# Extra products of other widths, addresses and tile forms behind the last product

## The chip, the cores and the metric

The kernel runs on one core of one Trainium2 chip. The core has five engines with a queue each: TensorE (PE for its matmuls, PEld for its weight loads), VectorE (DVE), ScalarE (ACT), GpSimd (POOL) and SyncE (SP, which issues all DMAs here). The metric is the time of one execution on the device in microseconds; the figure for a kernel is the median of its runs.

## The reference

Decayed linear attention over blocks, and then a two-layer network with a squared ReLU on the concatenated heads:

```python
batch, n_heads, seq, head_dim = (4, 8, 768, 64)      # attention
n_tokens, d_model, d_ff = (3072, 512, 2048)          # network
for b in range(nb):
    intra = np.einsum('bhic,bhjc->bhij', qb, kb) * Dmask[None]
    intra = np.einsum('bhij,bhjd->bhid', intra, vb)
    inter = np.einsum('bhid,bhde->bhie', qb * lam_pow[None], kv_state)
    out[:, :, sl] = intra + inter
    kv_state = lam_block[None, :, None, None] * kv_state + np.einsum('bhsd,bhse->bhde', kb_dec, vb)
...
h = x @ w_in
r = np.maximum(h, 0.0)
return ((r * r) @ w_out).astype(np.float32)
```

## The kernel before

The 3072 tokens are cut into 24 chunks of 128 (index t), and these into six groups of four (index m, 512 tokens). For each chunk the attention gives 512 features by 128 tokens; `split` stores them as a rounded part `xh` and a remainder `xl` in the tiles of the group, `xs_of[m]`. The network works on a group at a time: for each of the 16 slices f of the hidden layer, `hidden` makes 12 products into one PSUM tile (`wh` with `xh`, `wl` with `xh`, `wh` with `xl`, four blocks of 128 features each), `square` and `rest` make a rounded and a remaining part of the squared ReLU, and `project` makes 12 more products into the four accumulators of the group. Weights are held in `wh` and `wl`, 32 slots of 128 x 512 each, and both they and `xh`, `xl`, `gh`, `gl` have the type float32r. The attention's operands (`kv_sb`, `qk_sb`, `kv`, `a`, `mask`) are float32.

The order on each engine is that of the program text; nothing is rescheduled. In the main loop the attention of chunk t, which belongs to the next group, is spread over four slices: `scores` (line 304: 64 rows of the array for each head, two heads in different halves of the rows and different PSUM tiles), `masked`, then `attend` with `news` (line 335), `within` (line 343) and `before` (line 350), which use all 128 rows and 64 columns, two heads in different halves of the output partitions. `project` runs one slice behind `hidden`. So the last instructions of TensorE are those of `project` for the last slice of the last group: its products go two accumulators at a time (lines 428, 429, 433), and each finished accumulator is copied out by ScalarE (line 441) or VectorE (line 439) and sent by a DMA on SP (line 443). The body ends there (line 580); behind it comes the closing of the program, which the profile puts at line 630.

Other lines that are referred to: `warm` (line 65: products on a zeroed tile at the start, their results never read), `get_near` (line 248), `get_wide` (line 262) and `get_qpow` (line 278), which build tables at the start. Line 401 is the product of `hidden`.

PSUM has three pools here: `ps_acc` (four buffers, the accumulators), `ps_h` (two, the hidden slices), `ps_a` (two, named "att": scores and attention results). The last use of `ps_a` is the attention of chunk 23, in the next to last group.

Of the kernel before, what the change touches and what calls it, by code (L numbers as in the profile page):

```python
# [7 lines left out]
F32 = mybir.dt.float32  # L8
# [7 lines left out]
P = 128  # L16
B, H, S, D = 4, 8, 768, 64
# [4 lines left out]
DM = H * D  # L22
# [5 lines left out]
NM = NT // G  # L28
# [7 lines left out]
def body(ctx: ExitStack, tc: tile.TileContext, qT, kT, kvq, lam, w, out):  # L36
    nc = tc.nc
# [6 lines left out]
    ps_a = ctx.enter_context(tc.tile_pool(name="ps_a", bufs=2, space=PSUM))  # L44
    V = nc.vector
    rows = [slice(j * D, (j + 1) * D) for j in range(2)]
# [45 lines left out]
    wh = const.tile([P, 2 * NF, DM], F32R, name="wh")  # L92
# [5 lines left out]
    def w_out(f):  # L98
        return 2 * f + 2 if f < NF - 1 else 2 * NF - 1
# [97 lines left out]
    for p in range(NPR):  # L197
# [5 lines left out]
    mask = const.tile([P, 2, NPR, C], F32, name="mask")  # L203
# [5 lines left out]
        lambda o, x, y, op=op: V.tensor_tensor(out=o, in0=x, in1=y, op=op)  # L209
# [21 lines left out]
    for k in range(NS - 1):  # L231
        n = 1 << k
        x = (tr if k else s)[:, k : k + 1]
# [63 lines left out]
    xs_of = {}  # L297

    def scores(t, pool, name):
        sc_of[t] = [pool.tile([P, DM], F32, name=name) for _ in range(2)]  # L300
        k_, q_ = feat[t][:, 0], feat[t][:, 1]
        for p in range(NPR):
            for j, r in enumerate(rows):
                nc.tensor.matmul(  # L304
                    sc_of[t][j][:, p * C : (p + 1) * C], k_[r, p], q_[r, p],
                    start=True, stop=True, skip_group_check=True,
                )
# [83 lines left out]
                )  # L391


    g_of, accs, stage = {}, {}, []

    def hidden(m, f, xh, xl):
# [22 lines left out]
    def project(m, f):  # L419
        gh, gl = g_of.pop((m, f))  # L420
        if f == 0:
            accs[m] = [ps_acc.tile([P, DM], F32, name="acc") for _ in range(G)]
        end = f == NF - 1
        j = w_out(f)

        def high(i):
            cs = slice(i * C, (i + 1) * C)
            nc.tensor.matmul(accs[m][i], gh[:, cs], wh[:, j], start=f == 0, stop=False)  # L428
            nc.tensor.matmul(accs[m][i], gh[:, cs], wl[:, j], start=False, stop=False)  # L429

        def low(i):
            cs = slice(i * C, (i + 1) * C)
            nc.tensor.matmul(accs[m][i], gl[:, cs], wh[:, j], start=False, stop=end)  # L433
            if end:
                if i == 0:
                    stage.append(wk.tile([P, G, DM], F32, name="o", tag="raw"))
                o = stage[-1][:, i]
                if i % 2:
                    V.tensor_copy(o, accs[m][i])
                else:  # L440
                    nc.scalar.copy(o, accs[m][i])
                t = m * G + i
                nc.sync.dma_start(out=out[t * C : (t + 1) * C, :], in_=o)

        n = 2 if end and m == NM - 1 else 1
        for i in range(0, G, n):
            for step in (high, low):
                for k in range(i, i + n):
                    step(k)
# [81 lines left out]
    for m in range(NM):  # L531
        if m + 1 < NM:
            new_x(m + 1)
        for f in range(NF):
# [43 lines left out]
            if step == 0:  # L578
                scores(t, ps_a, "att")
    project(*prev)  # L580


def _limit():
# [50 lines left out]
```

## Time and profile before

| | |
|---|---|
| time, median of 2 runs | 636.02 us (635.94 to 636.09) |
| span of the profiled execution | 636.4 us |
| TensorE matmuls, busy | 624.6 us, 3744 instructions |
| TensorE weight loads, busy | 508.8 us, 3744 instructions |
| VectorE, ScalarE, GpSimd, busy | 222.1, 233.9, 88.5 us |
| DMA | 48.81 MB, of it 6.29 MB written to memory |

Times are in microseconds from the first instruction unless marked ns. A row of the groups of instructions has the line, engine, operation, output <- input by the program's names, the part of the array in use (rows*columns), the shape, the count, then busy time in us and the mean of one in ns, then the idle time before them and what ended it. Rows of the timeline and of the chain begin with a start and a length; "x12" counts merged instructions. The rows of one source line have the shortest, the median and the longest duration in ns, then the first and the last start. The chain is the work that ended last, followed back from the last instruction. A matmul's recorded duration reaches from its start until its result has left the array, and the next begins before that; so the cost of one in a row of matmuls is the distance from start to start.

### The profile page before, as it was taken

The page shows a single profiled execution, that of the slowest core. Times are in us where ns is not written, and L with a number is a line of the kernel's source. Part 1 is how long each engine was busy: PE and PEld are TensorE (multiplying, and loading weights), DVE is VectorE, ACT ScalarE, POOL GpSimd, SP SyncE. Part 2 cuts the span into 40 slices and gives each one's busy share as a digit, 9 for nine tenths or more (in the row PEclk, how much of TensorE's full clock was granted, in tenths as well). Part 3 has the DMA queues.
Part 4 walks back from the last instruction along what each step waited for, and adds up shares of the span by engine and source line. Part 5 has one row for each costly group of instructions (what it writes and reads, how often), then busy time and mean ns, then how long its engine had stood idle before and what let it go on. Part 6 is the DMA issues. An engine that isn't in the chain of part 4 may idle for free.

```text
span 636.4 us, 8960 instructions
## 1 busy us (share of the span) xinstructions
PE 624.6 (98%) x3744; PEld 508.8 (80%) x3744; DVE 222.1 (35%) x341; ACT 233.9 (37%) x383; POOL 88.5 (14%) x105
## 2 busy tenths in 40 slices
PE   8889999999999999999999999999999999999997
PEld 5768888888788888888888888888888888888885
DVE  6899999922222023121221221212312212211111
ACT  3277777723232324232323232323232323322232
POOL 4631222321010100210120010101201000000000
PEclk9799999999999999999999999999999999999999
DMA  8647576232021013010211202102302000100001
GB/s 310 253 134 239 161 261 205 96 131 67 1 66 52 17 67 106 27 67 2 67 57 76 67 1 76 58 1 67 122 11 67 1 2 0 67 1 1 0 1 66
DMA packets 18488, 48.81 MB, mean 77 GB/s; under 512 B 2064, under 2 KB 2064, under 8 KB 18448
## 3 DMA queue, kind: packets, MB, share of 16 engines
q1 hardware_dynamic: 18448, 48.24, 22.3%
q8 instruction: 29, 0.48, 0.3%
q14 instruction: 11, 0.09, 0.0%
HBM read 41.94 MB, written 6.29 MB: 76 GB/s over the span
## 4 chain that ended last, share of the span: by engine, by line
PE 95%; DVE 2%; DMA 1%; POOL 0%; issue 0%; ACT 0%; SPq 0%; DVEq 0%; POOLq 0%
PE h L401 40%; PE acc L428 14%; PE acc L429 14%; PE acc L433 14%; PE att L304 3%; PE att L343 3%; PE att L350 2%; PE att L335 2%; PE att L65 1%; DMA raw<-in_w 1%; DVE mask L288 1%; PE acc L304 0%; DVE A L152 0%; PE h L304 0%; PE h L248 0%
## 5 line engine op out<-in xcount | busy, mean ns | idle before, releaser
L416 DVE TENSOR_TENSOR gl<-h,gh 128x512 fp32r<-128x512 f32 x96 | 66.3, 691 | 395.8 <-ACT h L411 395.8
L408 ACT ACTIVATE h<-h 128x512 f32<-128x512 f32 x96 | 55.9, 582 | 346.8 <-PE h L401 346.7
L428 PE MATMUL acc<-wh,gh 128*128 128x512 f32 x384 | 151.7, 395 | 0.0
L429 PE MATMUL acc<-wl,gh 128*128 128x512 f32 x384 | 149.6, 390 | 0.0
L433 PE MATMUL acc<-wh,gl 128*128 128x512 f32 x384 | 149.0, 389 | 0.0
L401 PE MATMUL h<-xh,wh 128*128 128x512 f32 x384 | 105.3, 396 | 0.7 <-ACT xh L370 0.7
L401 PE MATMUL h<-xh,wl 128*128 128x512 f32 x384 | 103.0, 390 | 2.0 <-DVE wl L161 2.0
L401 PE MATMUL h<-xl,wh 128*128 128x512 f32 x384 | 102.6, 389 | 0.0
L428 PEld LDWEIGHTS acc<-wh,gh 128*128 128x128 f32 x384 | 72.1, 188 | 17.9 <-issue 2.1
L401 PEld LDWEIGHTS h<-xh,wl 128*128 128x128 f32 x384 | 72.0, 188 | 17.7 <-DVE wl L161 2.4
L433 PEld LDWEIGHTS acc<-wh,gl 128*128 128x128 f32 x384 | 72.1, 188 | 15.2
L401 PEld LDWEIGHTS h<-xl,wh 128*128 128x128 f32 x384 | 72.1, 188 | 15.0
L401 PEld LDWEIGHTS h<-xh,wh 128*128 128x128 f32 x384 | 70.5, 188 | 16.9 <-ACT xh L370 0.9
L429 PEld LDWEIGHTS acc<-wl,gh 128*128 128x128 f32 x384 | 72.1, 188 | 14.2
L410 ACT ACTIVATE gh<-h 128x512 fp32r<-128x512 f32 x96 | 57.6, 600 | 3.0
L411 ACT ACTIVATE h<-h 128x512 f32<-128x512 f32 x96 | 57.0, 594 | 0.0
L311 POOL TENSOR_TENSOR qk_sb<-qk_sb,qpow 128x512 f32<-128x512 f32 x18 | 23.3, 1295 | 200.9 <-PE att L304 200.9
L388 POOL TENSOR_TENSOR kvd<-kv,qpow 64x256 f32<-64x256 f32 x32 | 21.4, 668 | 155.9 <-DVE kv L360 86.6
L343 PE MATMUL att<-a,kv_sb 128*64 128x128 f32 x336 | 23.6, 282 | 2.5 <-DVE a L323 2.5
L323 DVE TENSOR_TENSOR a<-att,mask 128x512 f32<-128x512 f32 x40 | 25.6, 681 | 0.0
L122 ACT ACTIVATE A<-raw 128x1024 f32<-128x1024 f32 (+1 forms) x17 | 18.6, 1095 | 18.8 <-DMA raw<-in_w 15.5
L304 PEld LDWEIGHTS att<-qk_sb 64*128 64x128 f32 x320 | 19.4, 187 | 6.8 <-issue 6.7
(91 smaller groups left out, 385.3 us busy)
## 6 DMA issues: line engine op xcount, KB each, us to landing
raw<-in_w SPq DMA_DIRECT2D x32, 512.0 KB, 4.6
kv_sb<-in_kvq SPq DMA_DIRECT2D x22, 512.0 KB, 4.7
out_x<-o SPq DMA_DIRECT2D x24, 256.0 KB, 2.2
qk_sb<-in_kT SPq DMA_DIRECT2D x22, 256.0 KB, 2.6
qk_sb<-in_qT SPq DMA_DIRECT2D x22, 256.0 KB, 3.0
lent<-in_kvq SPq DMA_DIRECT2D x2, 512.0 KB, 7.6
lent<-in_kT SPq DMA_DIRECT2D x2, 256.0 KB, 7.9
lent<-in_qT SPq DMA_DIRECT2D x2, 256.0 KB, 7.3
```

Of the source, the lines that this page charges most:

```text
L304: nc.tensor.matmul(sc_of[t][j][:, p * C : (p + 1) * C], k_[r, p], q_[r, p], start=True, stop=True, skip_group_check=True,)
L311: nc.gpsimd.tensor_tensor(out=feat[t][:, 1], in0=feat[t][:, 1], in1=qpow, op=ALU.mult)
L323: V.tensor_tensor(out=a, in0=sc_of[t][j].rearrange("p (a b) -> p a b", a=NPR), in1=mask[:, j], op=ALU.mult,)
L343: nc.tensor.matmul(o[r, p * C : (p + 1) * C], tok[t][1][:, 2 * p + j, :], a[j][:, p, :], start=first and p == 0, stop=last, skip_group_che ...
L401: nc.tensor.matmul(h, wt[:, w_in(f), kt * P : (kt + 1) * P], x[:, kt], start=k == 0, stop=k == 11)
L408: nc.scalar.activation(h, h, AF.Relu)
L410: nc.scalar.activation(gh, h, AF.Square)
L411: nc.scalar.activation(h, h, AF.Square)
L416: V.tensor_tensor(out=gl, in0=r, in1=gh.bitcast(F32), op=ALU.subtract)
L428: nc.tensor.matmul(accs[m][i], gh[:, cs], wh[:, j], start=f == 0, stop=False)
L429: nc.tensor.matmul(accs[m][i], gh[:, cs], wl[:, j], start=False, stop=False)
L433: nc.tensor.matmul(accs[m][i], gl[:, cs], wh[:, j], start=False, stop=end)
```

## The change

A function `probes` is added and called once, behind the last `project`. It issues products on operands that lie in SBUF anyway: weights from `wh` (slot j, columns c to c + 127) with `xf[0]`, the `xh` of the last group seen as 128 x 2048; and, in the last loop, 64x64 blocks of `mask` with rows of `mask`. They write new "att" tiles, and nothing reads them. Every product starts its own result (start and stop both set).

```diff
+    def probes():
+        xf = [x.rearrange("p a b -> p (a b)") for x in xs_of[NM - 1]]
+        def lot(n, width, stationary, offset=0, rows_=slice(0, P), banks=1):
+            ts = [ps_a.tile([P, DM], F32, name="att") for _ in range(banks)]
+            for i in range(n):
+                j, c = stationary(i)
+                r = rows_[i % len(rows_)] if isinstance(rows_, list) else rows_
+                a = (i % 2) * DM + offset
+                nc.tensor.matmul(
+                    ts[i % banks][:, 0:width], wh[r, j, c : c + P], xf[0][r, a : a + width],
+                    start=True, stop=True, skip_group_check=True,
+                )
+        other = lambda i: (i % 32, i % 4 * P)
+        same = lambda i: (3, P)
+        lot(12, 512, other)
+        lot(12, 512, same)
+        lot(16, 256, other)
+        lot(12, 384, other)
+        lot(16, 128, other)
+        lot(12, 512, other, offset=256)
+        lot(12, 512, other, offset=32)
+        lot(16, 512, other, rows_=rows, banks=2)
+        lot(16, 256, other, rows_=rows, banks=2)
+        for width in (128, 256):
+            ts = [ps_a.tile([P, DM], F32, name="att") for _ in range(2)]
+            for i in range(32):
+                r, c = rows[i % 2], rows[i // 2 % 2]
+                nc.tensor.matmul(
+                    ts[i % 2][c, 0:width], mask[r, 0, i % 4, 0:D],
+                    mask[r, 0].rearrange("k p i -> k (p i)")[:, 0:width],
+                    start=True, stop=True, skip_group_check=True,
+                )
...
     project(*prev)
+    probes()
```

The nine calls of `lot` issue 124 products and the last loop 64, together 188. With `rows_=rows` a product uses 64 rows of the array, the lower and the upper half in turn, and writes two PSUM tiles in turn. In the last loop the row half changes with every product and the column half with every second, so that four products in a row use the four quarters of the array.

## The prediction

> **What bounds the kernel now.** The page comes first: span, busy shares, clock, and the shares of the chain that ended last.
>
> ```profile
> span 636.4 us, 8960 instructions
> PE 624.6 (98%) x3744; PEld 508.8 (80%) x3744; DVE 222.1 (35%) x341; ACT 233.9 (37%) x383; POOL 88.5 (14%) x105
> ...
> PEclk9799999999999999999999999999999999999999
> ...
> PE 95%; DVE 2%; DMA 1%; POOL 0%; issue 0%; ACT 0%; SPq 0%; DVEq 0%; POOLq 0%
> ...
> L428 PE MATMUL acc<-wh,gh 128*128 128x512 f32 x384 | 151.7, 395 | 0.0
> ```
>
> TensorE is busy for 98% of the span and makes up 95% of the chain. After the first slices its clock is granted in full. So one more matmul costs its place in the row of matmuls, unless it lies beside the tail of the program. The 395 ns of the L428 row is not that place: matmuls overlap. The chain in order of time gives the distance from one matmul to the next.
>
> ```profile
> 618.13 2.72 PE h L401 x12
> ...
> 623.57 2.72 PE h L401 x12
> ...
> 631.28 0.47 PE acc L433 x2
> ...
> 631.77 0.69 DVE o L439
> ```
>
> Twelve products of 512 columns take 2.72 us, which is 0.2267 us each. The timeline of the tail and the instructions of L630 (the end of the program) show what stands behind the last product.
>
> ```profile
> 630.79 2.43 SPq L443 DMA_DIRECT2D out_x<-o  x4
> ...
> 631.12 0.61 PE L433 MATMUL acc<-wh,gl 128*128 128x512 f32 x2
> 631.54 0.58 ACT L441 COPY o<-acc 128x512 f32<-128x512 f32 x1 [0.77 <-PE acc L433]
> 631.77 0.69 DVE L439 COPY o<-acc 128x512 f32<-128x512 f32 x1 [0.67 <-PE acc L433]
> ```
>
> ```profile
> L630 SPq EVENT_SEMAPHORE  x7: 17/28/2037, 633.3 to 636.3; - x7
> ...
> L630 SPq DRAIN  x3: 7/7/7, 635.6 to 635.9; - x3
> L630 PEldq DRAIN  x2: 13/1482/2952, 628.8 to 636.0; - x2
> ...
> L630 PEldq EVENT_SEMAPHORE  x2: 51/51/51, 635.8 to 636.3; - x2
> ```
>
> The last two products start at 631.12 and 631.35, so TensorE's next slot is 631.12 + 2 x 0.2267 = 631.57. After it come two copies, the output DMAs, and a 2037 ns wait of SP for their landing, with TensorE idle. SP's drain at 635.6 opens the closing handshake of all engines, which ends with the span at 636.4: 0.8 us. TensorE therefore has 635.6 - 631.57 = 4.0 us of free cover at the end.
>
> **The change part by part.** Nothing is removed or moved. No DMA, no VectorE, ScalarE or GpSimd instruction is added; nothing of SP's queue is passed. Behind project(*prev) stand 188 products in eleven lots, and on TensorE nothing is queued behind them but its closing drain. The operands (wh, the last xh, mask) were written long before, so no wait for another engine is expected.
>
> First, how many matmul instructions a product makes, and the price of those that are not 128x128 with 512 columns. The groups of instructions, the timeline of the start, one line's instructions and the granted clock:
>
> ```profile
> L343 PE MATMUL att<-a,kv_sb 128*64 128x128 f32 x336 | 23.6, 282 | 2.5 <-DVE a L323 2.5
> L304 PE MATMUL att<-qk_sb 64*128 64x128 f32 x320 | 23.2, 285 | 0.0
> ...
> L65 PE MATMUL att<-kv 128*128 128x512 f32 x8 | 6.6, 977 | 1.3 <-POOL kv L59 1.3
> ```
>
> ```profile
> 9.21 1.95 PE L248 MATMUL h<-pz 8*128 8x8 f32 x16
> 11.55 0.85 PE L262 MATMUL h<-near,move 128*128 128x64 f32 x6 [0.39 <-ACT near L252]
> 12.34 1.12 PE L278 MATMUL att<-blk,pz 8*128 8x512 f32 x2
> ```
>
> ```profile
> L262 PE MATMUL h<-near,move x6: 275/275/294, 11.6 to 12.1; 128*128 128x64 f32 x6
> ```
>
> ```profile
> L278 PE MATMUL att<-blk,pz x2: 587/640/692, 12.3 to 12.9; 8*128 8x512 f32 x2
> ```
>
> ```profile
> core 0: us, PE busy (x) PEld busy (x) DVE busy (x) ACT busy (x) POOL busy (x), PEclk, DMA share, GB/s
> ...
> 9.20:11.20 2.00, 1.96 (x17) 1.86 (x16) 1.81 (x3) 0.03 (x2) 0.00 (x0) 1.00 1.06 420
> 11.20:13.00 1.80, 1.45 (x8) 1.04 (x8) 0.68 (x4) 1.24 (x2) 0.00 (x0) 1.00 1.00 407
> 505.90:508.30 2.40, 2.40 (x49) 2.19 (x48) 0.51 (x1) 1.67 (x3) 0.00 (x0) 1.00 0.03 7
> ```
>
> L248 issues 8 float32 products and has 16 instructions, L278 one and has two: a float32 product is two passes. L428 has 384 for 384 float32r products: one pass. The lots on wh and xh are float32r (124 passes); the two on mask are float32 (64 products, 128 passes).
>
> Loads: at full clock (column PEclk, 1.00) the six passes of L262 with 128-column weights and 64 moving columns follow each other every (0.85 - 0.275)/5 = 0.115 us. So little streams there that the weight load sets the distance.
>
> Tiles: the L278 passes, alone in the array, start (1.12 - 0.587) = 0.53 us apart for 512 columns. With one load of 0.115 inside it that leaves 0.42, or 0.105 to 0.13 us per 128 columns. The chain shows the passes of half-width tiles:
>
> ```profile
> 506.02 0.62 PE att L335 x16
> 506.64 0.88 PE att L343 x16
> 507.51 0.87 PE att L350 x16
> ...
> 522.21 1.09 PE att L304 x16
> 523.30 2.95 PE h L401 x12
> ```
>
> L343 and L350 (128*64 tiles, 128 columns) take 0.0545 us per pass, half of a lone pass: two tiles run at once. L304 (64*128 tiles) takes 1.09 with a change of tile form at its head; without 0.22 for that it is again 0.0545. The change back shows as 2.95 against 2.72: 0.23. L335, 64 columns, gets down to 0.62/16 = 0.039, change of form included.
>
> Now the lots, each as count x distance:
>
> 1. Four lots of 12 with 512 columns (other weights; the same weights; column offsets 256 and 32): 48 x 0.2267 = 10.88 us. That equal weights save nothing has a row: L428 and the matmul after it use the same gh, and PEld still counts a load for every matmul (3744 and 3744). An offset costs nothing known; a dearer one would have to show against 0.2267.
> 2. 384 columns: 12 x 0.170 (three quarters of 0.2267) = 2.04. Bounds 0.115 (load) and 0.2267, so 1.4 to 2.7.
> 3. 256 columns: half of 0.2267 is 0.113, the load 0.115; as both nearly bind I take 0.120. 16 x 0.120 = 1.92. Bounds 1.8 and 3.6.
> 4. 128 columns: the load binds. 16 x 0.115 = 1.84. Bounds 0.0545 and 0.2267: 0.9 to 3.6. I stay with L262, the only row with a full array of weights and a short stream.
> 5. 64-row tiles, 512 columns, rows and banks alternating: no row has float32r in half-height tiles. If two run at once as in L304: 16 x 0.1133 = 1.81; if one at a time, 3.63. I take the first, since L304 has the same tile form and the same alternation.
> 6. The same with 256 columns: half the stream is 0.057, two loads at once by L304 at most 0.0545, so 0.060: 0.96; if one at a time 1.92.
> 7. 64x64 tiles, float32, 128 columns, 64 passes over four tiles: never seen here. Four at once: half of 0.0545, 64 x 0.0272 = 1.74. Two at once: 3.49. One: 64 x 0.105 = 6.7.
> 8. The same with 256 columns: 3.49 for four at once, 6.98 for two, 13.4 for one.
> 9. Two changes of tile form (before 5 and 7): 2 x 0.22 = 0.44. Bounds 0 and 1.
>
> For 7 and 8 the rows show two tiles wherever two are offered, and a full gain of two; nothing in them stops at two. So I take four at once, with two as the first rival. The Trainium skill (TensorEngine Tiling, Key Properties) says that tiles of one tiling load and multiply independently; by it 7 and 8 together are 5.2 us, by the two-tile rows taken as a ceiling 10.5. The two-tile rows agree with it and no row here shows four.
>
> Two things I set at nothing. Fifteen tiles go through the two "att" buffers, and a wait for the earlier user could stand before each: bound 0.16 (a 0.39 us matmul against its distance of 0.23) plus the 0.051 of a semaphore instruction, 15 x 0.21 = 3.2 us. I take 0 because the earlier user is TensorE itself, in order. And 504 more instructions have to be fetched; no row shows TensorE waiting for a fetch, so 0, and some 2 us if one is late (like the output's 2.0 us landing).
>
> Sum: 10.88 + 2.04 + 1.92 + 1.84 + 1.81 + 0.96 + 1.74 + 3.49 + 0.44 = 25.1 us. TensorE's last pass is then issued out at 631.57 + 25.1 = 656.7, leaves the pipeline 0.16 later, and the handshake adds 0.8: 657.65. The output DMAs landed 22 us earlier and cover nothing more. Against the span of 636.4 that is +21.2 us. The profiled span stands 0.4 us above the median of 636.02, so the time is 636.02 + 21.2 = 657.2 us, 3.3% more.
>
> **The rivals.**
> Two tiles at a time: a pass waits for the other pass of its own product, the next tile's is queued behind it, and only neighbours overlap. 7 and 8 cost 10.47 in place of 5.23. For it: every row has exactly two. Time 662.4.
> Half-height float32r products run one after the other: 5 and 6 rise by 2.78. Against it: L304. Time 660.0.
> Narrow float32r products cost as much as wide ones, 0.2267 each: 2, 3 and 4 rise by 0.68 + 1.71 + 1.79 = 4.2. The trace has no float32r product under 512 columns, so only the 512 row bounds it. Time 661.4.
> Issue binds: no pass follows another by less than the 0.0545 of L343, whatever its tile, in a burst of 128. Then 7 costs 3.49 and 8 stays: time 658.9. Against it: L335 at 0.039, though in bursts of 16. The Trainium skill (TensorE: Matmul & The Clock Gate, Back-to-back issue gap) names a bound of about 62 ns per matmul that holds when matmuls are decoded in software; by it 7 and 8 would be 7.9 us and the time about 659.9. The L335 row speaks against it.
> Not slower: the products are not executed because nobody reads them, or take no more than the 4.0 us cover behind 631.57. Then the time stays 636.0. Against it: L65 writes a tile nobody reads, and its 8 instructions are in the trace. To stay within 2% (12.7 us) the sum must come to 16.6 us or less; the four 512-column lots alone are 10.9.
>
> **How the numbers follow.** Four tiles at once 0.52; two at a time 0.22; half-height in turn 0.08; narrow at full price 0.07; issue 0.05; several of these together 0.03; not slower, or within 2%, 0.03. The predicted time is that of the likeliest, 657.2. The range runs from its low end (4 at 0.0545, -0.97, and 9 at nothing, -0.44: 655.8) to two tiles at a time with half-height in turn (665.2), rounded to 655.5 and 666. About 2% is what a measurement can tell from no change: slower by more than that 0.96, within it 0.03, faster 0.01, the last two from the final case.
>
> **What would show it.** Behind 631.57 the chain should consist of the lots on TensorE, 48 of them 0.2267 apart, the 128-column lot 0.115 apart, the 64-row lots 0.113 and 0.060, the mask lots 0.027 and 0.0545 per pass. The copies and output DMAs should stand where they stood, and from TensorE's drain to the end there should be 0.8 us. The forecast is wrong if the mask lots come to 0.0545 and 0.109, if an offset or a narrow width misses its distance, or if gaps stand between lots.

## The result, and the profile after

The changed kernel took 659.0 us (median of two runs, 658.43 and 659.57) against 636.02: slower by a factor of 1.0353, 95% interval 1.0314 to 1.0393. The forecast was 657.2 with a range from 655.5 to 666. On another chip, with more runs of both, it was 658.05 against 636.0 (ratio 1.0352, interval 1.033 to 1.0375). One of the four executions of the kernel with the lots ahead, below, took 809.9 us at a granted clock of 0.75; it is left out of the comparisons.

The page of the changed kernel, its span, busy shares, clock and the shares of the chain:

```profile
span 657.5 us, 9465 instructions
...
PE 649.7 (99%) x3996; PEld 530.0 (81%) x3996; DVE 223.7 (34%) x341; ACT 233.8 (36%) x383; POOL 89.9 (14%) x105
...
PEclk8989999999999999999999999999999999999999
...
PE 96%; DVE 3%; issue 0%; ACT 0%; POOL 0%; DVEq 0%; ACTq 0%; POOLq 0%
```

TensorE has 252 more matmuls and as many more loads: the 124 + 2 x 64 passes of the forecast. VectorE and ScalarE have the same counts as before. The products that nobody reads were executed.

The chain at the end, in order of time (start, length):

```profile
622.40 2.72 PE h L438 x12
...
630.56 20.20 PE att L405 x123
650.76 2.09 PE att L425 x59
...
652.86 3.72 PE att L425 x64
```

L438 is the old L401, moved by 37 lines; L405 and L425 are the lots. The chain ends in the lots, as forecast, and no longer in a copy. The engines' closing instructions (shortest/median/longest in ns, first and last start):

```profile
L668 SPq EVENT_SEMAPHORE  x8: 17/28/22216, 632.1 to 657.4; - x8
...
L668 PEldq DRAIN  x2: 13/785/1557, 655.1 to 657.1; - x2
```

SP waited 2.0 us for the last output before; now it waits 22.2 us more, for TensorE. TensorE's first drain ends at 655.1 + 1.557, about 656.6, the span at 657.5: 0.9 us, where 0.8 was assumed.

The stretches of the single lots (from the first product of one lot to the first of the next; busy us and records of TensorE, the granted clock, the DMA share):

```profile
core 0: us, PE busy (x), PEclk, DMA share, GB/s
630.40:635.84 5.44, 5.44 (x25) 1.00 0.52 197
635.84:637.75 1.91, 1.91 (x17) 1.00 0.00 0
637.75:639.84 2.09, 2.09 (x15) 1.00 0.00 0
639.84:641.57 1.73, 1.73 (x17) 1.00 0.00 0
641.57:647.26 5.69, 5.69 (x26) 1.00 0.00 0
647.26:649.42 2.16, 2.16 (x18) 1.00 0.00 0
649.42:650.71 1.29, 1.29 (x17) 1.00 0.00 0
650.71:652.85 2.14, 2.08 (x65) 1.00 0.03 8
652.85:656.58 3.73, 3.72 (x64) 1.00 0.00 0
```

| lots | forecast us | measured us |
|---|---|---|
| 512 columns, other and equal weights | 24 x 0.2267 = 5.44 | 5.44 |
| 256 columns | 1.92 | 1.91 |
| 384 columns | 2.04 | 2.09 |
| 128 columns | 1.84 | 1.73 |
| 512 with offsets 256 and 32 (and a change of tile form) | 5.44 + 0.22 | 5.69 |
| 64 rows, 512 columns | 1.81 | 2.16 |
| 64 rows, 256 columns (and a change) | 0.96 + 0.22 | 1.29 |
| 64x64, 128 columns | 1.74 | 2.14 |
| 64x64, 256 columns (with the way out of the array, 0.16) | 3.49 + 0.16 | 3.73 |
| sum | 25.3 | 26.2 |

The untiled lots came out at their forecast. The 0.9 us that is missing lies in the tiled ones, where one lot meets the next. The timeline shows the loads standing still there (start, length; in brackets the idle time before it and its releaser):

```profile
647.26 1.81 PEld L405 LDWEIGHTS att<-xh,wh 64*128 64x128 f32 x16 [0.37 <-issue]
649.41 1.14 PEld L405 LDWEIGHTS att<-xh,wh 64*128 64x128 f32 x16 [0.34 <-PE att L405]
...
650.71 1.84 PEld L425 LDWEIGHTS att<-mask 64*64 64x64 f32 x64 [0.16 <-PE att L405]
...
652.85 3.27 PEld L425 LDWEIGHTS att<-mask 64*64 64x64 f32 x64 [0.30 <-PE att L425]
```

Four pauses, where two changes of tile form had been charged; the second and the fourth stand where the form stays. The releaser tells the last three from the first: they end with a product of the lot before. In the trace the first load into each "att" tile of a lot waits for a semaphore, and the last product into the same PSUM buffer raises it. In the last three lots these loads start 0.056 to 0.067 us after the recorded end of that product, except the second load of the last lot, which comes 0.103 us behind it. So this is the wait for the earlier user of a buffer. It shows where a lot writes both "att" buffers up to its end. An untiled lot writes one, and the next lot takes the other, whose last product ended a lot earlier.

What a border costs can be read from the starts of the products (us; "last" reaches to the start of the next lot):

| lot | taken together | inside the lot | first | last |
|---|---|---|---|---|
| 64 rows, 512 columns | two products | 0.228 | 0.341 | 0.444 |
| 64 rows, 256 columns | two products | 0.118 | 0.225 | 0.334 |
| 64x64, 128 columns | four passes | 0.109 | 0.161 | 0.440 |
| 64x64, 256 columns | four passes | 0.216 | 0.267 | |

Inside the lots the distances are those of the forecast. With 0.10 us at the end of the untiled lot before them, the four borders cost about 0.21, 0.35, 0.28 and 0.38 us, together 1.2 us, of which 0.44 had been charged.

### The profile page after: what moved, and what is told of

The parts are those of the page before. It is cut to its first block, busy times and chain, and to the rows that moved or that the text cites. A ratio compares the mean times of both kernels' runs of the same rounds, so it can differ in the third digit from the quotient of the medians.

```text
span 657.5 us, 9465 instructions
## 1 busy us (share of the span) xinstructions
PE 649.7 (99%) x3996; PEld 530.0 (81%) x3996; DVE 223.7 (34%) x341; ACT 233.8 (36%) x383; POOL 89.9 (14%) x105
## 4 chain that ended last, share of the span: by engine, by line
PE 96%; DVE 3%; issue 0%; ACT 0%; POOL 0%; DVEq 0%; ACTq 0%; POOLq 0%
PE h L438 40%; PE acc L465 14%; PE acc L466 13%; PE acc L470 13%; PE att L304 3%; PE att L405 3%; PE att L343 3%; PE att L350 2%; PE att L335 2%; PE att L65 1%; PE att L425 1%; DVE wl L161 1%; DVE a L323 1%; PE acc L304 0%; DVE A L146 0%
## 5 line engine op out<-in xcount | busy, mean ns | idle before, releaser
L438 PE MATMUL h<-xh,wh 128*128 128x512 f32 x384 | 105.3, 396 | 0.7 <-ACT xh L370 0.7
L438 PE MATMUL h<-xh,wl 128*128 128x512 f32 x384 | 103.7, 392 | 2.2 <-DVE wl L161 2.2
L438 PE MATMUL h<-xl,wh 128*128 128x512 f32 x384 | 103.5, 391 | 0.0
L438 PEld LDWEIGHTS h<-xh,wl 128*128 128x128 f32 x384 | 72.3, 189 | 18.0 <-DVE wl L161 2.6
L438 PEld LDWEIGHTS h<-xl,wh 128*128 128x128 f32 x384 | 72.6, 189 | 15.2
L438 PEld LDWEIGHTS h<-xh,wh 128*128 128x128 f32 x384 | 70.5, 188 | 16.9 <-ACT xh L370 0.9
L388 POOL TENSOR_TENSOR kvd<-kv,qpow 64x256 f32<-64x256 f32 x32 | 22.2, 695 | 155.0 <-DVE kv L360 85.7
L168 POOL COPY mark<-wl 1x1 f32<-1x1 f32 x15 | 14.3, 953 | 66.4 <-DVE wl L161 62.6
```

What stands on the lines that cost most here:

```text
L438: nc.tensor.matmul(h, wt[:, w_in(f), kt * P : (kt + 1) * P], x[:, kt], start=k == 0, stop=k == 11)
```

## The experiments

All edits are shown against the changed kernel. None changes what is computed for the output. The runs from "Which tiles run at once" on are one execution each, and only their profiles are read. To compare whole runs free of the start, each profile is read from the start of the last `hidden` (the row before the last slice of `project`) to the end of the span: 636.4 - 623.57 = 12.8 us before and 657.5 - 622.40 = 35.1 us after, 22.3 us more.

**The change again.**

> The changed kernel once more, beside the kernel before on the same chip. The first profile has 26.2 us from the first added product (630.40) to the last one's end (656.6), and 0.9 us to the end of the span; the profile of before has 4.8 us from the slot behind its last product to its end. The theory of the cover (C: the lots cost their length less what the output's way home hides, about 4 us) expects spans 26.2 + 0.9 - 4.8 = 22.3 us apart; the first comparison had 23.0 between the medians. Rival S: the 0.7 us beyond it, and the 1.8 us by which the forecast was short, lie in the lots or at the end; then the spans of the two kernels are 23 us apart or more. Rival U: they lie in the start of the profiled execution of before, which was longer than in its timed runs; then the spans of the timed runs of before are near 634.

Five runs, 657.43 to 660.77 us; 17 runs of before, 635.34 to 637.99 us with spans from 633.3 to 635.9. Last `hidden` of this profile:

```profile
620.28 2.72 PE h L438 x12
```

From there to the end of the span (655.4) are 35.1 us, again 22.3 more than before. So S falls: the part behind the last `hidden` is 22.3 us longer in both profiles, as C says. U holds: a time is its span plus 2.1 us (657.43 and 655.4 in this profiled run, 635.34 and 633.3 in one of before), so the profile of before with its 636.4 belongs to an execution of about 638.5, above all 17. Timed runs can start as slowly: before took 638.61 us (span 636.5) beside a later run on a different chip. Where the profile lost time shows between 13.0 and 24.5 us. The same stretch of before, of this run and of the first profile after (length; busy us and records of TensorE, its loads, VectorE, ScalarE and GpSimd; then the granted clock, the DMA share and GB/s):

```profile
13.00:24.50 11.50, 9.01 (x92) 7.44 (x92) 10.45 (x14) 4.35 (x8) 6.80 (x7) 0.56 0.94 360
```

```profile
13.00:24.50 11.50, 10.85 (x160) 9.19 (x162) 11.27 (x17) 4.57 (x8) 9.45 (x9) 0.85 1.04 412
```

```profile
13.00:24.50 11.50, 9.62 (x146) 8.27 (x144) 11.30 (x15) 4.27 (x8) 7.37 (x8) 0.87 1.01 384
```

TensorE had 0.56 of its clock there in the profile of before, 0.85 and 0.87 in the other two, and 160 and 146 matmuls in place of 92. The first profile after has one more stretch at the lower clock, where the other two have 1.00:

```profile
24.50:48.00 23.50, 20.30 (x174) 15.88 (x174) 22.62 (x29) 14.76 (x19) 12.09 (x11) 0.93 0.46 147
```

Behind that nothing differs. One `hidden` early in the main loop starts, before and after, at

```profile
83.99 2.72 PE h L401 x12
```

```profile
82.82 2.72 PE h L438 x12
```

and the last one at 623.57 and 622.40: 539.58 us later in both. So the spread of some 3 us between runs of one kernel comes from the start, where TensorE waits and its clock is halved for a varying time. The clock alone doesn't measure it: the profile of the lots twice, below, has 0.76 and 0.93 in these two stretches, and its last `hidden` still starts only 0.4 us later than in this run. The Trainium skill (TensorE: Matmul & The Clock Gate, The HAM clock gate) ties the clock to TensorE's activity in windows that run freely against the program. Three different shares, 0.56, 0.85 and 0.87, in the same stretch agree with free-running windows; what counts as activity these rows don't show.

**Lots ahead of the last project.**

```diff
-    project(*prev)
-    probes()
+    probes()
+    project(*prev)
```

> The lots stand before the last project instead of behind it, so the output's way home lies behind everything again. C expects the whole length of the lots, 26.2 us and a change of tile form (0.2), over the kernel before: about 4 us more than the changed kernel. Rival N (the tail hides nothing, and the 23.0 us are the lots' own cost): the same time as the changed kernel.

Ratio to before 1.0417, interval 1.039 to 1.0444: 26.5 us on 636.0. The profile (span 662.7) has the last `hidden` at

```profile
623.44 2.72 PE h L438 x12
```

which leaves 39.3 us to the end, 26.4 more than before and 4.2 more than the changed kernel. That is C. N falls: the same lots cost 4 us more when the output's way home isn't beside them.

**The lots twice.**

```diff
     probes()
+    probes()
```

> The lots are issued twice, one after the other. C expects the changed kernel plus 26.2 us (and 0.2 for a change of tile form), since the cover of 4 us is spent once: about 49 over the kernel before. Rival N: twice the 23.0, 46 over the kernel before.

Ratio 1.0761, interval 1.0742 to 1.078: 48.4 us. In the profile (span 682.2) the last `hidden` starts at

```profile
620.71 2.72 PE h L438 x12
```

and 61.5 us follow, 48.7 more than before: 22.3 + 26.4. The cover is spent once. N's 46 lies below the interval (47.2 to 49.6).

**Only the first lot.**

```diff
         lot(12, 512, other)
-        lot(12, 512, same)
...
-                nc.tensor.matmul(
-                    ts[i % 2][c, 0:width], mask[r, 0, i % 4, 0:D],
...
```

> Only the first lot of twelve 512-column products is left, 12 x 0.2267 = 2.7 us, less than the 4.0 us of cover. C expects no change against the kernel before (within 0.3 us). Rival N: 2.7 us slower.

Ratio 1.001, interval 0.9997 to 1.0024 over 12 runs: 0.6 us, between -0.2 and 1.5. The 2.7 us of N are outside. In the profile (span 634.1) the last `hidden` starts at

```profile
621.15 2.72 PE h L420 x12
```

and 12.95 us follow, 0.1 more than before, though twelve more products ran.

**Which tiles run at once.** All lots are replaced by six sets of 64 float32 passes (256 columns) that differ in the order of tiles alone.

```diff
+        for place in (
+            lambda i: (i % 2, i // 2 % 2), lambda i: (i % 2, 0), lambda i: (0, i % 2),
+            lambda i: (0, 0), lambda i: (i // 8 % 2, i // 16 % 2), lambda i: (i // 2 % 2, i % 2),
+        ):
+            quarters(256, place)
```

> In place of the lots six sets of 32 float32 products in 64x64 tiles, 256 columns (64 passes each): (1) all four quarters in turn as in the change, (2) two row halves in one column half, (3) two column halves in one row half, (4) one quarter alone, (5) each quarter eight times before the next, (6) all four with the column half changing first. Theory Q (four quarters run at once, a pass of a quarter alone takes 0.21 us): 3.5, 6.9, 6.9, 13.6, 13.6, 3.5 us. Rival P (a pass is held up by something else than its tile, so that 0.055 is the least distance of two passes): (1) and (6) stay at 3.5, (2) and (3) come to about the same 3.5, and only (4) and (5) are longer.

The six stretches (start to end, length; busy us and records of TensorE and of its loads; granted clock, DMA share, GB/s):

```profile
629.28:633.03 3.75, 3.68 (x64) 2.34 (x65) 1.00 0.75 277
633.03:640.21 7.18, 7.16 (x65) 5.50 (x65) 1.00 0.01 3
640.21:647.16 6.95, 6.95 (x64) 4.51 (x65) 1.00 0.01 2
647.16:660.98 13.82, 13.82 (x67) 8.51 (x65) 1.00 0.00 0
660.98:671.78 10.80, 10.80 (x65) 7.14 (x66) 1.00 0.01 2
671.78:676.26 4.48, 4.42 (x68) 2.53 (x62) 1.00 0.00 0
```

One quarter alone takes 0.216 us per pass, two 0.109 to 0.112, four 0.0587: each quarter works on its own. P, with a least distance of 0.055 that would have held (2) and (3) at 3.5, falls; with four quarters three of four passes start 0.006 to 0.007 us behind the one before. Two sets miss Q's numbers. Set 5 took 10.8 in place of 13.6: although each quarter comes eight times before the next, passes of neighbouring groups ran together where the quarter changes, so that their starts don't keep the order of the program text. By whom they were brought into that order was not tried. Set 6 took 4.48 in place of 3.5, with Q's distances once four are under way; the rest lies at its start, where the last passes of set 5 still run and a load waits for the tile that they write.

The run also tests the border between lots without a change of tile form. The row of its waits has the total in us, the number of times and the longest:

```profile
PEld att L416 <- PE att L416: 1.5, 3, 0.5
```

The loads waited for an earlier product of the lots three times: before sets 2 and 3, whose forerunners write both buffers to their end, and at the start of set 6. Sets 3 and 4 write one buffer each, and the loads of sets 4 and 5 begin without a pause. So it is the buffer, and not the tile form or a new lot as such, that makes these pauses.

**Widths.** Ten lots of 16 products, 512 to 16 columns, then 128 and 16 columns on one block of weights.

```diff
+        for width in (512, 448, 384, 320, 256, 224, 192, 128, 64, 16):
+            lot(16, width, other)
+        lot(16, 128, same)
+        lot(16, 16, same)
```

> In place of the lots ten lots of 16 float32r products with a 128x128 weight block each and 512, 448, 384, 320, 256, 224, 192, 128, 64 and 16 columns, then 16 with 128 and 16 with 16 columns on one and the same block. Theory L (distance = the longer of the load, 0.112, and the stream, columns/2.4 per us plus 0.0134): 0.227, 0.200, 0.173, 0.147, 0.120, 0.112, 0.112, 0.112, 0.112, 0.112 us, and the same 0.112 with equal blocks because each is loaded again. Rival M (the extra 0.013 is a share of the stream, 6%): 0.198, 0.170, 0.142, 0.113 for 448 to 256 columns. Rival E (an equal block isn't loaded again): the last two lots at 0.067 and 0.02.

The stretches with 384, 256, 224 and 16 columns, then the two with an equal block (length; busy us and records of TensorE; granted clock, DMA share, GB/s, here and below):

```profile
634.22:637.02 2.80, 2.80 (x18) 1.00 0.00 0
...
639.36:641.27 1.91, 1.91 (x18) 1.00 0.00 0
641.27:643.05 1.78, 1.78 (x18) 1.00 0.00 0
...
648.34:650.12 1.78, 1.78 (x18) 1.00 0.04 9
650.12:652.34 2.22, 2.22 (x19) 0.81 0.00 0
652.34:655.86 3.52, 3.52 (x17) 0.50 0.00 0
```

Divided by 16: 0.2025, 0.175, 0.146, 0.119 for 448 to 256 columns, then 0.109 to 0.112 from 224 down to 16. L holds, with a fixed share beside the stream and the load as the floor; M is 0.004 to 0.007 short in each. The last two lots, on an equal block, fit no theory: from the second to the twelfth product they are 0.109 to 0.114 apart, then 0.213. E is out. The clock column tells the two parts from each other: it fell to 0.50 at 651.5 us, between them.

**Equal blocks.** Whether it was the equal block after all:

```diff
+        for stationary in (same, other, pair, same, other):
+            lot(32, 128, stationary)
+        lot(32, 256, same)
+        lot(32, 256, other)
```

> In the run with the widths, products of 128 and 16 columns on one block of weights went from 0.112 to 0.213 us apart after the thirteenth. Here lots of 32 with 128 columns on one block, on other blocks each time, on two blocks in turn, on one block again, on other blocks again; then 32 with 256 columns on one block and on other blocks. Theory B (an equal block can't be loaded beside the product that uses it, so load and stream add up): 0.21 in the first and fourth lot after some products, 0.112 in the others, more than 0.120 with 256 on one block. Rival Z (it was the end of the program that slowed them): 0.112 in the first five lots, 0.120 in the sixth.

The second stretch (other blocks), then the fourth and the sixth (equal block):

```profile
633.36:636.93 3.57, 3.57 (x34) 1.00 0.02 5
...
640.50:644.08 3.58, 3.58 (x35) 1.00 0.00 0
...
647.65:651.54 3.89, 3.89 (x34) 1.00 0.00 0
```

0.110 to 0.112 with equal and with other blocks, 0.1217 at 256 columns. B falls. Z's numbers hold, but not its cause: this program ends without a slower stretch, so an end of a program doesn't slow products by itself. Its clock stayed at 1.00 in all lots.

**Half-height products.**

```diff
+        lot(16, 512, other, rows_=rows, banks=2)
+        lot(16, 512, other, rows_=[rows[0]], banks=2)
+        lot(16, 256, other, rows_=rows, banks=2)
+        lot(16, 256, other, rows_=[rows[0]], banks=2)
+        lot(16, 128, other, rows_=rows, banks=2)
+        lot(16, 128, other, rows_=[rows[0]], banks=2)
```

> In place of the lots six lots of 16 float32r products in 64-row tiles: 512 columns with the row halves in turn, 512 with the lower half alone (two PSUM tiles in turn in both), then the same two with 256, and with 128 columns. The change had 0.117 and 0.060 us per product at 512 and 256 with the halves in turn. Theory H (two halves run at once): 0.117 and 0.227 at 512, 0.060 and 0.120 at 256, 0.056 and 0.112 at 128. Rival K (a 64-row product is shorter by itself): 0.117 at 512 also with the lower half alone.

The first two stretches (busy us and records of TensorE and of its loads):

```profile
628.73:630.90 2.17, 2.12 (x16) 1.42 (x17) 1.00 0.96 368
630.90:634.68 3.78, 3.78 (x16) 2.88 (x17) 1.00 0.18 69
```

With the lower half alone 0.236 per product at 512 columns and 0.125 at 128; with the halves in turn 0.136 and 0.074. K falls, H holds, but both kinds carry about 0.2 to 0.4 us more per lot, which in 16 products is 0.01 to 0.02 each. All six lots have the same tile form and write both buffers, and the loads wait for a product of the lot before again:

```profile
PEld att L405 <- PE att L405: 0.9, 3, 0.5
```

**Addresses.** Two runs, mostly with 512 columns, in which the first column of the moving operand changes.

```diff
+        for offset in (0, 32, 256, 8, 128, 480):
+            lot(32, 512, other, offset=offset)
+        for offset in (0, 32, 256):
+            lot(32, 512, same, offset=offset)
```

> In place of the lots six lots of 32 float32r products with 512 columns whose column offsets are 0, 32, 256, 8, 128 and 480, all with other blocks of weights, then three with one block and offsets 0, 32 and 256. The first profile has distances of 0.225 to 0.238 us with offsets 256 and 32 where offset 0 has 0.2267. Theory O (the address of the moving columns makes it dearer): 0.227 with 0, about 0.232 with 32 and with the offsets that are no multiple of 512, also on one block. Rival W (the address of the weights against that of the columns): as O with other blocks, but 0.227 in the last three lots. Rival T (it comes from another transfer or engine at that moment): all nine at 0.227.

Offsets 0, 32 and 256, then 32 on one block of weights:

```profile
628.25:635.50 7.25, 7.25 (x33) 1.00 0.39 148
635.50:642.96 7.46, 7.46 (x33) 1.00 0.00 0
642.96:650.23 7.27, 7.27 (x34) 1.00 0.00 0
...
679.72:687.17 7.45, 7.45 (x33) 1.00 0.00 0
```

Divided by 32: 0.2267, 0.2331, 0.2272, 0.2328; the equal block with offset 0 has 0.2271. O holds, also on one block, so W falls, and T with it: it is the address of the columns. But an offset that is no multiple of 512 is not enough, as 256 shows.

```diff
+        for offset in (0, 64, 384, 96, 192, 4, 0):
+            lot(24, 512, other, offset=offset)
+        for offset in (0, 32, 128):
+            lot(24, 256, other, offset=offset)
```

> Offsets so far: 0.2267 us with 0, 0.227 with 128 and 256 after three to eight products, 0.233 with 8, 32 and 480. Here 24 products of 512 columns each with offsets 0, 64, 384, 96, 192, 4, 0, then 24 of 256 columns with 0, 32 and 128. Theory A (the start must be a multiple of 128 columns, 512 bytes): 0.227 with 384 and 0, 0.233 with 64, 96, 192 and 4; at 256 columns 0.120, 0.123, 0.120. Rival F (of 64 columns): 64 and 192 at 0.227 as well.

Offsets 64, 96 and 192:

```profile
634.02:639.46 5.44, 5.44 (x26) 1.00 0.00 0
...
644.90:650.49 5.59, 5.59 (x26) 1.00 0.00 0
650.49:655.94 5.45, 5.45 (x25) 1.00 0.00 0
```

Divided by 24, 64 and 192 are at 0.2267 and 0.227, as is 384; 96 is at 0.233 and 4 at 0.2316. That is F: the start must be a multiple of 64 columns (256 bytes). A falls with 64 and 192. As the width is a multiple of 64 in all these lots, the end shifts with the start, and the two were not told apart. With 256 columns no offset was dearer (0.119 to 0.120 from product to product), which neither had expected of 32.

## Why the prediction was right

- What bounds: right. The lots lie on TensorE, one after the other, and the chain ends in them.
- The cover of 4.0 us behind the last product: shown three ways, by 2.7 us of products that cost nothing, by 4.2 us more without the cover, and by a second set of lots at its full 26.4 us.
- The untiled lots: right to 0.11 us each, the load floor from L262 included. The widths run shows why: the longer of 0.112 for the load and the stream with a fixed 0.013.
- Equal weights for nothing: right, also at 128 columns, where a saved load would have shown.
- Offsets at nothing: off by 12 x 0.0064 = 0.08 us, for offset 32 alone.
- Four quarters at once: right. The first rival, two at a time, would have made 10.5 us of the last two lots; they took 5.9.
- Half-height float32r products: right (two at once, 0.114 and 0.059 us per product inside the lots).
- The wait between lots for a buffer is the term that was wrong. The prediction named it, bounded it at 0.21 us for a tile, and took 0 "because the earlier user is TensorE itself, in order". TensorE did wait for its own last products, at three borders, which cost 0.35, 0.28 and 0.38 us. Of this the last products of the two half-height lots lose 0.22 us each, the prediction's bound for one tile, and those of the first mask lot 0.33; the rest lies at the heads of the new lots. As it came at three borders and not at fifteen tiles, it made 1.0 us, less than the bound of 3.2.
- Step 9, two changes of tile form at 0.22 each: the first border cost 0.21 us as charged, though the second load there also waits for a buffer. The second change stands at a border with a wait, and there it shows nothing of its own: 0.28 us, less than at the two borders where the form stays. What was charged for it covered part of the waits by luck.
- Of the 0.9 us by which the sum was short, 0.35 lie in the 512-column half-height lot, 0.11 in the next and 0.40 in the 64x64 lot with 128 columns.
- Two of the prediction's own signs of being wrong are there, gaps between lots and an offset that misses its distance. Both are small against the 22.3 us.
- From the sum to the time: the forecast added 21.2 us to the median; the two profiles, read from the last `hidden`, differ by 22.3: 0.9 more in the lots, and 0.1 more behind them. What the two first runs have beyond 636.02 + 22.3 = 658.3 is within the spread of the start, 657.43 to 660.77 for the same kernel. The step "the profiled span stands 0.4 us above the median" compared unlike things: a time is its span plus 2.1 us, and the profile of before was of a slow start. It did little harm because the sum was made from the last product on, where the start doesn't enter.
- Nothing shows a wait for instructions that were fetched late: right, TensorE is busy for 26.11 of 26.18 us. Busy time doesn't show the waits for a buffer, because a product counts as busy until its result has left the array.

## What to carry to other kernels

The price of work on the engine that bounds is read from distances between starts, never from durations, and work behind the last product is free only up to the output's way home, here 4 us. An engine that works in order still waits for its own results: a set of products that writes all buffers of a PSUM pool up to its end holds up the first load of the next set, here at 0.3 to 0.4 us a border, while sets that took the buffers in turn paid nothing. Whether a third buffer would save it in the half-height lots was not tried. Where two profiles of a kernel differ by a few us, look first at the granted clock of their first tens of us, and compare from a landmark behind it.

## What was not expected of the hardware

A moving operand of 512 float32r columns that doesn't start on a multiple of 64 columns (256 bytes) of its tile costs 2 to 3% (0.2316 to 0.2334 for 0.2267 us, with offsets 4, 8, 32, 96 and 480). In the two runs on addresses the first three to seven products of some lots at a multiple of 64 were slower as well (0.2315 to 0.232 us on average): those with offsets 128, 192, 256 and 0, which stand behind a lot with a dear offset. Those with offsets 64 and 384, behind a lot at a multiple of 64, were not. So this goes with the lot before and not with the lot's own offset.

TensorE's clock fell to 0.50 in the widths run without any pause of TensorE, after the lots of 64 and 16 columns, and the distance of products went from 0.112 to 0.213. In the run with equal blocks 160 products of 128 columns in a row (17.8 us) didn't lower it. So the gate seems to judge how much streams through the array, not whether instructions follow each other; that short streams were the cause is argued from these two runs and was not tried alone. The start doesn't decide it: in all twelve profiles the clock fell to a half between 11.1 and 14.3 us, with TensorE busy for 85 to 89% of the 3.4 us before, so that short streams (8 and 64 columns, lines 248 and 262) and short pauses lie together there.
